# Two MLPs whose 512-column matmuls read the moving operand as two interleaved streams

## The chip, the cores and the metric

The kernel runs on one core of a Trainium2 chip. The metric is the device time of one execution in microseconds (us); the median of three runs is given. A row of the profile belongs to one profiled execution.

## The reference

Sink-and-window attention over 2 batches, 8 heads, 768 positions and 64 channels gives 1536 tokens of 512 features. Two MLPs follow, each with its own weights, 512 to 2048 to 512:

```python
x = attention(q, k, v, n_sink, window)          # (1536, 512)
h = x @ w_in;  g = h * clip(h + 3, 0, 6) / 6;  x = g @ w_out       # first MLP
h = x @ w_in2; g = h / (1 + exp(-1.702 * h));  out = g @ w_out2    # second MLP
```

All inputs and the output are float32.

## The kernel before, in words

[...] To keep the precision, each operand is split into a high part (a rounded copy) and a low part (the rest), and each product is made of three matmuls: high by high, high by low, low by high. The helper `copy` (lines 428 to 432) makes high parts on ScalarE or VectorE; the subtractions for low parts are at lines 517, 579, 637 and 850.

Tokens are taken in blocks of 512 and the 2048 hidden features in 16 pieces of 128. One *item* is one block with one piece. `up` (line 524) multiplies the block's activations by a piece of W_in: 4 chunks of 128 input features with 3 matmuls each, at line 536, into one PSUM bank of 128 hidden features by 512 tokens. The activation and the split into `gh` and `gl` follow. `down` (line 587) multiplies the result by a piece of W_out, 4 times 3 matmuls at line 604. So an item has 24 matmuls, each with a stationary operand of 128 by 128 and a moving operand of 128 by 512. There are 48 items in each MLP, 96 in all, which makes 2304 such matmuls.

What moves and what stands still differs. In `up` of both MLPs, W_in is stationary and the activations `xyh`/`xyl` (tokens along the columns) move. In `down` of the first MLP, W_out is stationary and `gh`/`gl` move, so that tokens stay along the columns. In `down` of the second MLP, `gh`/`gl` are stationary and W_out moves, so that tokens come out along the partitions and features along the columns, ready for the store at line 649. Before the change each moving operand is read from its first column to its last.

Each weight arrives as a float64, seen as two 32-bit words, and is put together as float32 by one ScalarE instruction (line 448) and four VectorE instructions (lines 453, 461, 469, 476), a piece (128 by 1024) at a time. Each piece of the first MLP's weights is kept in `wf` and replaced by the second's while the last block of the first MLP runs.

The order on every engine is written by a planner (`Plan`, line 284). Each operation has prices in ns, one for each engine that may do it, a due time and its dependencies; `issue` (line 354) places operations one after the other by start time, price and due time, and lets casts and copies fall to ScalarE or VectorE. For three matmuls of 512 columns its price is

```python
[("PE", 3 * (n / 2.4 + 13.3))]
```

that is 226.6 ns a matmul. In the fast path, the due times of successive items lie 5440 ns apart (times 1.6 or 1.25 for the first 24), at line 907. At the start of the program the attention's operations share the engines with the first items.

Of the kernel before, what the change touches and what calls it, by code (L numbers as in the profile page):

```python
# [17 lines left out]
P = 128  # L18
# [11 lines left out]
RATE_DMA = 340  # L30
# [15 lines left out]
DOWN = 7000  # L46
START = 3000
RATE = 1.6
RATE2 = 1.25
# [14 lines left out]
def tile_sink_window_attention_moe_moe2(  # L64
# [13 lines left out]
    NF = w1.shape[0]  # L78
# [349 lines left out]
    def copy(eng, out, in_):  # L428
        if eng is nc.scalar:
            eng.copy(out, in_)  # L430
        else:
            eng.tensor_copy(out, in_)  # L432

    def halves(t0, n):
        return range(t0 // 256, (t0 + n) // 256)

# [46 lines left out]
    def plan_mlps(plan, blocks, item_due):  # L483
# [40 lines left out]
        def up(i):  # L524
            which, t0, n, f = items[i][:4]
            wh, wl = split(i, 0)
            h = Buf(cls="bank", kind="h")
            s, o = divmod(t0, 512)
            for c in range(NC):

                def mm(e, c=c):
                    xh, xl = xyh[s][:, c, o : o + n], xyl[s][:, c, o : o + n]
                    cols = slice(c * P, (c + 1) * P)
                    prods = ((wh.tile[:, cols], xh), (wh.tile[:, cols], xl), (wl.tile[:, cols], xh))
                    for k, (w, x) in enumerate(prods):
                        e.matmul(  # L536
                            h.tile[:, :n], w, x, start=(c == 0 and k == 0), stop=(c == NC - 1 and k == 2)
                        )

                xs = [b for half in halves(t0, n) for b in plan.x[half][c]]  # L540
                plan.op([("PE", 3 * (n / 2.4 + 13.3))], mm, due[i], reads=[wh, wl] + xs, writes=[h], chain="up")
            u, gh, gl = (Buf(cls=x) for x in ("u", "gh", "gl"))
            big = n == 512
            after = due[i] + (2600 if big else 1300)
            if which == 1:
                plan.op(
                    [("ACT", 585 if big else 370)],
                    lambda e: e.activation(u.tile[:, :n], h.tile[:, :n], AF.Relu, bias=three, scale=1.0),  # L548
                    after, reads=[h], writes=[u],
                )  # L550
                plan.op(
                    [("DVE", 602 if big else 335)],
                    lambda e: e.scalar_tensor_tensor(  # L553
                        out=u.tile[:, :n], in0=u.tile[:, :n], scalar=6.0, in1=h.tile[:, :n],
                        op0=ALU.min, op1=ALU.mult,
                    ),
                    after, reads=[h], writes=[u],
                )
            else:
                plan.op(  # L560
                    [("ACT", 478)],
                    lambda e: e.activation(u.tile[:, :n], h.tile[:, :n], AF.Sigmoid, scale=1.702),  # L562
                    after, reads=[h], writes=[u],
                )
                plan.op(
                    [("DVE", 602)],
                    lambda e: e.tensor_tensor(
                        out=u.tile[:, :n], in0=h.tile[:, :n], in1=u.tile[:, :n], op=ALU.mult
                    ),
                    after, reads=[h], writes=[u],  # L570
                )
            plan.op(
                [("ACT", 520 if big else 307), ("DVE", 335 if big else 200)],
                lambda e: copy(e, gh.tile[:, :n], u.tile[:, :n]),
                after, reads=[u], writes=[gh],
            )
            plan.op(
                [("DVE", 602 if big else 335)],
                lambda e: e.tensor_tensor(  # L579
                    out=gl.tile[:, :n], in0=u.tile[:, :n], in1=gh.tile[:, :n].bitcast(F32), op=ALU.subtract  # L580
                ),
                after, reads=[u, gh], writes=[gl],
            )
            g[i] = (gh, gl)
            wo[i] = split(i, 1)

        def down(i):
            which, t0, n, f, begin, end = items[i]
            wh, wl = wo.pop(i)
            gh, gl = g.pop(i)  # L590
            if begin:
                ys["b"] = [Buf(cls="bank", kind="y") for _ in range(4)]
            for e4 in range(4):
                yb = ys["b"][e4]

                def mm(e, e4=e4, yb=yb):
                    col = slice(e4 * P, (e4 + 1) * P)
                    if which == 1:
                        a, b = wh.tile[:, col], wl.tile[:, col]
                        prods = ((a, gh.tile), (b, gh.tile), (a, gl.tile))  # L600
                    else:
                        prods = ((gh.tile[:, col], wh.tile), (gh.tile[:, col], wl.tile), (gl.tile[:, col], wh.tile))
                    for k, (l, r) in enumerate(prods):
                        e.matmul(yb.tile, l, r, start=(begin and k == 0), stop=(end is not None and k == 2))  # L604

                plan.op(
                    [("PE", 3 * (n / 2.4 + 13.3))], mm, due[i] + DOWN,
                    reads=[wh, wl, gh, gl], writes=[yb], chain="down",
                )
                if end == "aside":  # L610
                    keep = Buf(cls="aside")
                    kept_y[t0, e4] = keep
                    plan.op(
                        [("ACT", 478), ("DVE", 602)], lambda e, yb=yb, keep=keep: copy(e, keep.tile, yb.tile),
                        due[i] + 5200, reads=[yb], writes=[keep],
                    )
                elif end == "y":
                    result(which, t0, e4, yb, due[i] + 5200)

        def result(which, t0, e4, yb, when):  # L620
            if which == 1:
                s = t0 // 512
                hi, lo = xyh[s][:, e4, :], xyl[s][:, e4, :]
                his = [plan.x[half][e4][0] for half in halves(t0, 512)]
                los = [plan.x[half][e4][1] for half in halves(t0, 512)]
                if (t0, e4) in kept_y:
                    part, psum = kept_y[t0, e4], yb
                    plan.op(
                        [("DVE", 602)],
                        lambda e: e.tensor_tensor(out=part.tile, in0=psum.tile, in1=part.tile, op=ALU.add),  # L630
                        when, reads=[psum], writes=[part],
                    )
                    yb = part
                plan.op([("ACT", 478)], lambda e: e.mul(hi, yb.tile, 1.0 / 6.0), when, reads=[yb], writes=his)
                plan.op(
                    [("DVE", 602)],
                    lambda e: e.scalar_tensor_tensor(
                        out=lo, in0=yb.tile, scalar=1.0 / 6.0, in1=hi.bitcast(F32), op0=ALU.mult, op1=ALU.subtract,
                    ),
                    when, reads=[yb] + his, writes=los,  # L640
                )
            else:
                o = Buf(cls="u")
                plan.op(
                    [("ACT", 478), ("DVE", 602)], lambda e: copy(e, o.tile, yb.tile), when, reads=[yb], writes=[o]
                )
                r = t0 + e4 * P
                plan.op(
                    [("SP", 262144 / RATE_DMA)], lambda e: e.dma_start(out=out[r : r + P, :], in_=o.tile), when,
                    reads=[o], chain="dma",  # L650
                )

# [214 lines left out]
    def fast_path():  # L867
        with tc.manual_schedule(), tc.tile_pool(name="mlp", bufs=1) as pool, tc.tile_pool(
# [34 lines left out]
            def item_due(items):  # L903
                t, due = RAMP0 + first * RAMP + START, []
                for n in range(len(items)):
                    due.append(t)
                    t += 5440 * (RATE if n < 8 else RATE2 if n < 24 else 1)
                return due

            plan_attention(plan, ap, pair_due)  # L910
# [3 lines left out]
    def general_path():  # L914
        with ExitStack() as st:
# [75 lines left out]
            with tc.manual_schedule():  # L991
                pool = st.enter_context(tc.tile_pool(name="gmlp", bufs=1))
                psum = st.enter_context(tc.tile_pool(name="gpsum", bufs=1, space=PSUM))
                plan = Plan()
                mlp_rings(plan, pool, psum)
                plan.limit = lambda b, slots, o: b.kind == "y" or H_BANKS > sum(
                    1 for x in slots if x is not None and (x.left or x in o.new) and x.kind == "h"
                )
                plan_mlps(
                    plan, [(s * 512, 0, NF) for s in range(NBLK)], lambda items: [5200 * n for n in range(len(items))]  # L1000
                )
                plan.issue()

# [69 lines left out]
```

## Time and profile before

| | us |
|---|---|
| median of 3 runs | 623.67 |
| lowest, highest of the runs | 622.96, 623.98 |
| profiled execution, first to last instruction | 622.8 |
| TensorE busy in it | 605.6 |
| weight loads busy (they overlap the matmuls) | 500.4 |
| VectorE busy | 501.1 |
| ScalarE busy | 261.2 |
| DMA, share of the 16 engines' span (main queue) | 23.6% |

The profiled execution's time is given by its span alone, 622.8 us, 0.9 us under the median of the runs. Busy time on TensorE overstates its work, since matmuls are pipelined: one lasts about 390 ns from its start to its modelled end, and the next starts well before that. The distance from one start to the next has to be read from counts over a stretch or from the chain of waits.

### The profile page before, as it was taken

How to read it: one execution, taken by the hardware profiler on the slowest of the kernel's cores; microseconds unless marked ns; L12 is line 12 of the kernel's file. 1: busy time of each engine (PE TensorE's matmuls, PEld its weight loads, DVE VectorE, ACT ScalarE, POOL GpSimd, SP SyncE). 2: the span in 40 equal slices, each digit the busy share in tenths (PEclk: the TensorE clock that was granted, in tenths of full speed). 3: DMA queues.
4: the chain of work that ended last, by engine and by line, in shares of the span. 5: the costliest groups of instructions: out<-in, count | busy, mean ns of one | idle time of the engine just before them, and what ended most of it. 6: DMA issues, size and time to landing. Idle time of an engine off the chain costs nothing.

```text
span 622.8 us, 10596 instructions
## 1 busy us (share of the span) xinstructions
PE 605.6 (97%) x4242; PEld 500.4 (80%) x4242; DVE 501.1 (80%) x1061; ACT 261.2 (42%) x553; POOL 1.4 (0%) x10
## 2 busy tenths in 40 slices
PE   7889999999999999999999999999999999999996
PEld 6777887777888888888888888888888888888885
DVE  7799999899956686799999999966666666666753
ACT  5897887767546321164443554312311012211111
POOL 0000000000000000000000000000000000000000
PEclk8899999999999999999999999999999999999999
DMA  8974442554400000003343334000100000100001
GB/s 264 374 228 145 160 165 86 174 170 175 157 1 2 1 1 1 0 2 135 136 144 129 132 130 141 1 0 1 69 1 1 0 1 0 69 0 1 0 1 72
DMA packets 11175, 50.91 MB, mean 82 GB/s; under 512 B 1456, under 2 KB 1456, under 8 KB 7024
## 3 DMA queue, kind: packets, MB, share of 16 engines
q1 hardware_dynamic: 11120, 50.18, 23.6%
q8 instruction: 35, 0.57, 0.4%
q14 instruction: 20, 0.16, 0.1%
HBM read 47.02 MB, written 3.15 MB: 81 GB/s over the span
## 4 chain that ended last, share of the span: by engine, by line
PE 78%; DVE 13%; ACT 3%; DMA 3%; issue 2%; POOL 0%; ACTq 0%; SPq 0%; POOLq 0%
PE bank L536 37%; PE bank L604 36%; DMA stage<-in_w_dram 2%; DVE pexp L764 2%; DVE wf L476 2%; DVE wf L469 2%; PE bank L800 2%; PE bank L749 1%; ACT pexp L772 1%; DVE u L553 1%; PE bank L823 1%; DVE wf L453 1%; PE bank L831 1%; DVE wf L461 1%; DVE w1l L517 1%
## 5 line engine op out<-in xcount | busy, mean ns | idle before, releaser
L536 PE MATMUL bank<-xyh,w0h 128*128 128x512 f32 x384 | 151.8, 395 | 2.3 <-DVE u L553 1.5
L536 PE MATMUL bank<-xyl,w0h 128*128 128x512 f32 x384 | 149.6, 390 | 1.0 <-DVE xyl L850 1.0
L536 PE MATMUL bank<-xyh,w0l 128*128 128x512 f32 x384 | 149.7, 390 | 0.0
L562 ACT ACTIVATE u<-bank 128x512 f32<-128x512 f32 x48 | 28.7, 599 | 173.2 <-PE bank L536 173.2
L536 PEld LDWEIGHTS bank<-xyh,w0h 128*128 128x128 f32 x384 | 72.1, 188 | 17.9 <-DVE u L553 2.1
L536 PEld LDWEIGHTS bank<-xyl,w0h 128*128 128x128 f32 x384 | 72.1, 188 | 15.5 <-DVE xyl L850 1.3
L536 PEld LDWEIGHTS bank<-xyh,w0l 128*128 128x128 f32 x384 | 72.1, 188 | 15.4 <-DVE w0l L517 0.3
L604 PE MATMUL bank<-gh,w1h 128*128 128x512 f32 x192 | 76.4, 398 | 0.0
L604 PE MATMUL bank<-gh,w1l 128*128 128x512 f32 x192 | 74.9, 390 | 0.7 <-DVE w1l L517 0.7
L604 PE MATMUL bank<-gl,w1h 128*128 128x512 f32 x192 | 75.0, 390 | 0.1
L604 PE MATMUL bank<-w1h,gl 128*128 128x512 f32 x192 | 74.8, 390 | 0.0
L604 PE MATMUL bank<-w1l,gh 128*128 128x512 f32 x192 | 74.7, 389 | 0.0
L604 PE MATMUL bank<-w1h,gh 128*128 128x512 f32 x192 | 74.7, 389 | 0.0
L432 DVE CAST w0h<-wf 128x512 fp32r<-128x512 f32 x81 | 34.3, 424 | 46.4 <-PE bank L536 46.4
L517 DVE TENSOR_TENSOR w0l<-wf,w0h 128x512 fp32r<-128x512 f32 x96 | 66.2, 689 | 5.1 <-PE bank L604 0.5
L579 DVE TENSOR_TENSOR gl<-u,gh 128x512 fp32r<-128x512 f32 x96 | 66.2, 689 | 1.9
L517 DVE TENSOR_TENSOR w1l<-wf,w1h 128x512 fp32r<-128x512 f32 x96 | 66.1, 689 | 1.0
L548 ACT ACTIVATE u<-bank,three 128x512 f32<-128x512 f32 x48 | 33.0, 687 | 72.5 <-PE bank L536 72.3
L432 DVE CAST w1h<-wf 128x512 fp32r<-128x512 f32 x61 | 26.0, 426 | 33.1 <-PE bank L604 33.0
L772 ACT ACTIVATE pexp<-pexp,nb 128x196 f32<-128x196 f32 x96 | 43.2, 452 | 12.4 <-DVE nb L764 12.2
L448 ACT ACTIVATE wf<-stage 128x1024 f32<-128x1024 f32 x32 | 36.9, 1152 | 18.1 <-DMA stage<-in_w_dram 16.2
L430 ACT CAST gh<-u 128x512 fp32r<-128x512 f32 x47 | 29.2, 622 | 35.8 <-DVE u L553 19.8
(93 smaller groups left out, 834.8 us busy)
## 6 DMA issues: line engine op xcount, KB each, us to landing
stage<-in_w_dram SPq DMA_DIRECT2D x32, 1024.0 KB, 4.9
wf<-in_kq_dram SPq DMA_DIRECT2D x8, 520.0 KB, 11.1
vc<-in_vc_dram SPq DMA_DIRECT2D x12, 320.0 KB, 4.6
out_dram<-u SPq DMA_DIRECT2D x12, 256.0 KB, 2.0
vb<-in_v_dram SPq DMA_DIRECT2D x10, 256.0 KB, 6.3
kq<-in_kq_dram SPq DMA_DIRECT2D x4, 520.0 KB, 10.9
vb<-in_v_dram SPq DMA_DIRECT2D x4, 128.0 KB, 6.5
par_i<-in_params_dram SPq DMA_DIRECT2D x1, 2.0 KB, 2.9
```

Source lines behind the costliest of these rows:

```text
L430: eng.copy(out, in_)
L432: eng.tensor_copy(out, in_)
L448: lambda e: e.activation(w.tile.bitcast(F32), top.bitcast(F32), AF.Abs),
L469: lambda e: e.scalar_tensor_tensor(out=w.tile, in0=top, scalar=-0x40000000, in1=w.tile, op0=ALU.bitwise_and, op1=ALU.bitwise_or),
L476: lambda e: e.scalar_tensor_tensor(out=w.tile, in0=low, scalar=29, in1=w.tile, op0=ALU.logical_shift_right, op1=ALU.bitwise_or),
L517: lambda e: e.tensor_tensor(out=lo.tile, in0=src.tile.bitcast(F32)[:, cols], in1=hi.tile.bitcast(F32), op=ALU.subtract),
L536: e.matmul(h.tile[:, :n], w, x, start=(c == 0 and k == 0), stop=(c == NC - 1 and k == 2))
L548: lambda e: e.activation(u.tile[:, :n], h.tile[:, :n], AF.Relu, bias=three, scale=1.0),
L562: lambda e: e.activation(u.tile[:, :n], h.tile[:, :n], AF.Sigmoid, scale=1.702),
L579: lambda e: e.tensor_tensor(out=gl.tile[:, :n], in0=u.tile[:, :n], in1=gh.tile[:, :n].bitcast(F32), op=ALU.subtract),
L604: e.matmul(yb.tile, l, r, start=(begin and k == 0), stop=(end is not None and k == 2))
L772: lambda e, n=n: e.activation(pes[n].tile[:, :W], pes[n].tile[:, :W], AF.Exp, bias=nbs[n].tile, scale=-1.0, accum_out=z.tile[:, n : n + 1],),
```

## The change: two streams

Every matmul of the MLPs reads its 512 moving columns in another order: 0, 256, 1, 257, 2, 258, and so on. The number of columns, the instructions, the tiles and the stationary operands stay. The output is still written from the first column of the bank to the last, so its columns come out in the order of the reading.

Three such readings (`up`, `down` of the first MLP, `up` of the second) put the tokens of a block into another order: place 8r + l holds token 64l + r. The store of each 128-by-512 result writes partition 8h + l to row 64l + 16q + h of the block for the q-th of its four results, in rows of 2 KB as before. In the second MLP's `down` it is the features that come out in the order of the reading, and the host has laid W_out's columns apart for that: even columns first, odd columns after. The planner's price of a matmul falls from n/2.4 + 13.3 to n/2.4 + 2.7 ns, and the distance of the due times from 5440 to 5184 ns (5200 to 5184 in the general path, which doesn't run with these inputs).

```diff
+    def woven(x):
+
+        return x.rearrange("p (a n) -> p n a", a=2)
...
-                            h.tile[:, :n], w, x, start=(c == 0 and k == 0), stop=(c == NC - 1 and k == 2)
+                            h.tile[:, :n], w, woven(x), start=(c == 0 and k == 0), stop=(c == NC - 1 and k == 2)
...
-                plan.op([("PE", 3 * (n / 2.4 + 13.3))], mm, due[i], reads=[wh, wl] + xs, writes=[h], chain="up")
+                plan.op([("PE", 3 * (n / 2.4 + 2.7))], mm, due[i], reads=[wh, wl] + xs, writes=[h], chain="up")
...
-                        e.matmul(yb.tile, l, r, start=(begin and k == 0), stop=(end is not None and k == 2))
+                        e.matmul(yb.tile, l, woven(r), start=(begin and k == 0), stop=(end is not None and k == 2))
...
-                    [("PE", 3 * (n / 2.4 + 13.3))], mm, due[i] + DOWN,
+                    [("PE", 3 * (n / 2.4 + 2.7))], mm, due[i] + DOWN,
...
-                r = t0 + e4 * P
+                rows = out[t0 : t0 + 512, :].rearrange("(l q h) d -> q h l d", l=8, q=4)[e4]
                 plan.op(
-                    [("SP", 262144 / RATE_DMA)], lambda e: e.dma_start(out=out[r : r + P, :], in_=o.tile), when,
+                    [("SP", 262144 / RATE_DMA)],
+                    lambda e: e.dma_start(out=rows, in_=o.tile), when,
...
-                    t += 5440 * (RATE if n < 8 else RATE2 if n < 24 else 1)
+                    t += 5184 * (RATE if n < 8 else RATE2 if n < 24 else 1)
...
+    def apart(w):
+
+        return w.reshape(-1, w.shape[1] // 2, 2).transpose(0, 2, 1).reshape(w.shape)
...
-        "w2": by_tile(x["moe2_w_in"], x["moe2_w_out"]),
+        "w2": by_tile(x["moe2_w_in"], apart(x["moe2_w_out"])),
```

## Rows read from the trace of the kernel before

**Rows 1.** Stages: length, each engine's busy us (instructions), clock, DMA share, GB/s

```profile
40.00:147.93 107.93, 103.54 (x1156) 84.10 (x1151) 105.31 (x265) 82.98 (x204) 0.00 (x0) 1.00 0.47 155
290.00:400.00 110.00, 110.00 (x486) 90.55 (x485) 109.05 (x167) 50.99 (x74) 0.00 (x0) 1.00 0.35 123
400.00:616.12 216.12, 216.12 (x955) 178.97 (x954) 144.78 (x264) 35.42 (x59) 0.00 (x0) 1.00 0.03 10
```

**Rows 2.** TensorE's waits, 147 to 617 us: total us, times, longest

```profile
PE bank L536 <- ACT pts L430: 0.2, 1, 0.2
```

**Rows 3.** Chain of waits, 400 us to the end: start, us, what

```profile
525.02 2.72 PE bank L604 x12
...
531.83 4.76 PE bank L536 x21
...
616.12 2.19 DMA out_dram<-u
```

**Rows 4.** Timeline of one `up` chunk and one `down` triple: start, us, what

```profile
608.50 0.39 PE L536 MATMUL bank<-xyh,w0h 128*128 128x512 f32 x1
608.51 0.19 PEld L536 LDWEIGHTS bank<-xyl,w0h 128*128 128x128 f32 x1
608.73 0.39 PE L536 MATMUL bank<-xyl,w0h 128*128 128x512 f32 x1
...
609.18 0.39 PE L604 MATMUL bank<-w1h,gh 128*128 128x512 f32 x1
```

**Rows 5.** Eight attention transposes of 128 columns (line 800): length, PE, weight loads, clock

```profile
53.25:54.12 0.87, 0.87 (x8) 0.79 (x7) 1.00 0.00 0
```

**Rows 6.** Matmuls of line 536, stages of the whole kernel

```profile
40.00:147.93 107.93, 41.54 (x156) 28.29 (x157) 1.00 0.47 155
147.93:211.81 63.88, 29.32 (x109) 19.86 (x110) 1.00 0.17 62
211.81:290.00 78.19, 44.02 (x178) 33.22 (x178) 1.00 0.05 17
290.00:400.00 110.00, 60.83 (x244) 45.19 (x242) 1.00 0.35 123
400.00:616.12 216.12, 122.29 (x468) 87.84 (x468) 1.00 0.03 10
```

**Rows 7.** Matmuls of line 604, the same stages

```profile
40.00:147.93 107.93, 39.00 (x144) 26.04 (x144) 1.00 0.47 155
147.93:211.81 63.88, 28.62 (x108) 20.05 (x108) 1.00 0.17 62
211.81:290.00 78.19, 41.99 (x168) 31.55 (x168) 1.00 0.05 17
290.00:400.00 110.00, 60.41 (x242) 45.37 (x243) 1.00 0.35 123
400.00:616.12 216.12, 126.25 (x487) 91.13 (x486) 1.00 0.03 10
```

**Rows 8.** VectorE's casts, 290 to 400 us, by line and form

```profile
L432 DVE CAST w0h<-wf 128x512 fp32r<-128x512 f32 x17 | 7.2, 422 | 0.0
...
L432 DVE CAST w1h<-wf 128x512 fp32r<-128x512 f32 x6 | 2.6, 426 | 0.0
...
L432 DVE CAST gh<-u 128x512 fp32r<-128x512 f32 x3 | 1.3, 422 | 0.0
```

**Rows 9.** Who waits for TensorE, 400 to 616 us: total us, times, longest

```profile
ACT u L562 <- PE bank L536: 164.7, 40, 5.6
DVE w0h L432 <- PE bank L536: 32.9, 23, 2.0
DVE w1h L432 <- PE bank L604: 30.6, 16, 2.9
```

**Rows 10.** The end of the timeline: start, us, what

```profile
616.12 3.23 SPq L649 DMA_DIRECT2D out_dram<-u  x4
...
617.12 0.39 PE L604 MATMUL bank<-w1h,gl 128*128 128x512 f32 x1
618.41 0.59 ACT L430 COPY u<-bank 128x512 f32<-128x512 f32 x1 [0.96 <-DMA out_dram<-u]
```

**Rows 11.** DMA issues of the page, stores: count, KB each, us to landing

```profile
out_dram<-u SPq DMA_DIRECT2D x12, 256.0 KB, 2.0
```

More of the change, by code (lines that the diff above doesn't have):

```diff
@@ L999, in general_path @@
                 plan_mlps(
-                    plan, [(s * 512, 0, NF) for s in range(NBLK)], lambda items: [5200 * n for n in range(len(items))]
+                    plan, [(s * 512, 0, NF) for s in range(NBLK)], lambda items: [5184 * n for n in range(len(items))]
                 )
```

## The prediction

> **What bounds the kernel now.** I begin with the busy time by stages. TensorE is busy without a break from 290 us to 616 us, VectorE in 109.05 of 110 us of the one stage and in 144.78 of 216.12 us of the next [rows 1]. A busy TensorE proves little, because a matmul's 390 ns overlap the next one's. So the second view is TensorE's waits: from 147 us to 617 us it waited 0.2 us in all [rows 2]. The third is the chain of waits over the same time. It runs through TensorE's matmuls alone, and its pieces give the distance between two matmuls: 2.72 us for 12 and 4.76 us for 21, both 226.7 ns [rows 3]. The fourth, the timeline, shows the same 0.22 to 0.23 us between neighbours, and each weight load starting beside the matmul before the one that it serves and lasting 0.19 us [rows 4]. The reader is to see that for 468 us (147.93 to 616.12) nothing but the number of matmuls and their distance sets the end. Before that it is different: from 40 us to 147.93 us VectorE is busy for 105.31 of 107.93 us, with TensorE at 103.54 [rows 1]. That stage ends when VectorE is done with attention and weights.
>
> **What could be taken off a matmul.** [...]
>
> The trace has one other dense row of full-height matmuls, the attention's transposes at the same clock: 8 in 0.87 us, 108.8 ns for 128 columns [rows 5]. [...]
>
> **Part by part.** (1) *The order of reading.* [...] No row shows neighbouring columns 1 KB apart, so a loss can't be excluded either: its upper bound is taken from the slowest pace per column that a full-height matmul shows, the transposes' 108.8 / 128 = 0.85 ns, which gives 435 ns for 512 columns, 208 ns more than now. [...]
>
> [...]
>
> (2) *Where the gain counts.* From 147.93 us on, lines 536 and 604 have 109 + 178 + 244 + 468 and 108 + 168 + 242 + 487 matmuls, 2004 together [rows 6, 7]. At 11.2 ns each that is 22.4 us, all on the path. Between 40 and 147.93 us there are 156 + 144 = 300, worth 3.4 us at most, but VectorE sets that stage: the bounds are 0 and 3.4 us, and I take 0.8 us, nearer to none, since VectorE has 2.6 us of air there [rows 1, 6, 7].
>
> (3) *What is late next.* The same items now want their VectorE work in less time. From 290 us to 400 us TensorE's 486 matmuls shrink by 5.4 us to 104.6 us, while VectorE is busy for 109.05 us: a shortfall of 4.4 us if nothing moves. What can move: 26 casts on VectorE there, 11.1 us in all, may go to ScalarE, which is busy for 50.99 of 110 us [rows 1, 8]; and conversions of the second MLP's weights can slip beyond 400 us, where VectorE is idle for a third of the time and its casts wait for TensorE, 32.9 and 30.6 us [rows 1, 9]. The planner knows both ways, and its due times and price go down with the change. So the give-back lies between 0 and 4.4 us; I take 1.2 us. After 400 us an item's 5.44 us holds 3.6 us of VectorE work (67%), and 5.17 us still hold it.
>
> (4) *Stores, layout, planner.* The stores move the same 12 times 256 KB in rows of 2 KB, and land 2.0 us after issue [rows 11]. Only the last ones are on the path: 5.7 us lie between the start of the last matmul (617.12) and the end (622.8) [rows 10]. The scattered rows need one more dimension in the access pattern; if each of the four last stores took half its landing time longer and they overlapped, that is 1 us, and I take 0, keeping 0 to 1 us. The first eight stores hide behind the matmuls; nothing queues behind them on SP but the later ones. The host's layout is outside the timed program. No instruction, tile or wait is added. The planner will place another order in the first 148 us; I allow 1.5 us either way for it.
>
> **The sum.** 22.4 + 0.8 − 1.2 = 22.0 us. The profiled execution's 622.8 us becomes 600.8 us; the median of the runs lies 0.9 us above that execution's span, so the time is 601.7 us.
>
> **The rivals.** [...]
>
> [...]
>
> *A partial cure.* Half of the 11.2 ns goes: 11.6 us on the path, some 612.5 us. [...]
>
> *VectorE takes over.* The matmuls reach 215.4 ns, but all of the 4.4 us come back between 290 and 400 us and the planner loses 1.5 us early: 606.4 us. The casts in [rows 8] speak against it.
>
> **Chances and range.** Full cure 0.68 (601.7 us), VectorE taking over 0.06 (606.4), partial cure 0.06 (612.5), no change 0.07 (623.7), slower 0.13. For one launch of this kernel 0.2% is 1.2 us, about what its runs can tell from no change. Faster 0.80, same 0.06, slower 0.14 (a part of the no-change case falls out on the slow side through the planner). The range: the low end has the full 22.4 + 3.4 us and 1 us of the planner's, 623.7 − 26.8 = 596.9, say 597; the high end takes in the partial cure, 613. It leaves out no change and slower, 0.20.
>
> **What would show it.** Right: the chain of waits has 12 matmuls in about 2.59 us; TensorE's waits after 148 us stay under 2 us; the stage in which the second weights are converted holds VectorE near 100%, with fewer casts on it; transposes stay at 109 ns. [...] The prediction fails above all if the reading of columns 1 KB apart has a price of its own.

## The result, and the profile after

The changed kernel takes 616.9 us (median, 615.9 to 618.6); the kernel before took 623.8 us beside it. The ratio is 0.9899, 95% interval 0.9875 to 0.9922: faster by some 7 us, where 22 us were forecast, and outside the range of 597 to 613 us. The profiled execution spans 614.0 us against 622.8 us. Each run's time lies 1.8 to 1.9 us above its span, so the execution profiled before would have been some 624.6 us, an estimate, and longer than any of the four timed beside it, while that of after was the shortest of its runs; the two traces therefore differ by 8.8 us, more than the medians do.

The reading itself did what was forecast. The chain of waits of the changed kernel, late in the program (start, length, what), answers to [rows 3]:

```profile
519.07 2.59 PE bank L608 x12
525.54 4.53 PE bank L540 x21
```

12 matmuls in 2.59 us and 21 in 4.53 us are 215.8 ns each, 10.9 ns less than before; 215.4 had been forecast. From 410 us to the start of the last matmul TensorE works without a break, busy for all of 196.75 us with 914 matmuls, 215.3 ns each with the edges included. But the stage in which the second MLP's weights are converted shows another picture. By stages (length, then PE, weight loads, VectorE, ScalarE), before and after; the first fence is of the kernel before, cut at 410 us to match:

```profile
290.00:410.00 120.00, 120.00 (x530) 98.84 (x529) 116.45 (x180) 52.13 (x75) 0.00 (x0) 1.00 0.32 112
```

```profile
290.00:410.00 120.00, 116.66 (x519) 95.71 (x518) 118.81 (x173) 58.25 (x78) 0.00 (x0) 1.00 0.33 114
```

In these 120 us the changed kernel starts 519 matmuls, fewer than the 530 of before. At 215.8 ns there is room for 556: 37 matmuls, 8.0 us, are lost. The waits of that stage (who for whom: total us, times, longest) say to whom:

```profile
PEld bank L608 <- DVE gl L583: 8.7, 17, 0.9
PE bank L608 <- DVE gl L583: 2.6, 10, 0.5
PEld bank L608 <- ACT gh L430: 1.0, 4, 0.3
```

TensorE waits for VectorE's `gl`, again and again. And on VectorE two instructions have grown. These are the instructions that read or write the staged weights from 260 us on (ns: least, median, most), first in the kernel before, then in the changed one:

```profile
L448 ACT ACTIVATE wf<-stage x16: 1137/1150/1167, 267.4 to 388.8; 128x1024 f32<-128x1024 f32 x16
L469 DVE SCALAR_TENSOR_TENSOR wf<-stage,wf x16: 1218/1224/1230, 277.9 to 394.8; 128x1024 int32<-128x1024 int32 x16
L476 DVE SCALAR_TENSOR_TENSOR wf<-stage,wf x16: 1217/1224/1231, 280.2 to 396.2; 128x1024 int32<-128x1024 int32 x16
```

```profile
L452 ACT ACTIVATE wf<-stage x16: 1427/1619/1707, 265.5 to 401.8; 128x1024 f32<-128x1024 f32 x16
L473 DVE SCALAR_TENSOR_TENSOR wf<-stage,wf x16: 1495/1522/1589, 277.3 to 409.6; 128x1024 int32<-128x1024 int32 x16
L480 DVE SCALAR_TENSOR_TENSOR wf<-stage,wf x16: 1425/1509/1581, 281.8 to 411.6; 128x1024 int32<-128x1024 int32 x16
```

Nobody edited these lines. They have one thing in common: they take every second 32-bit word out of `stage`. The other costly instructions of both engines kept their durations within some 2% (the subtraction for `w0l` 689 and 688 ns, the sigmoid 599 and 598). In the same changed trace, before the first MLP matmul at 42 us, they still have the old length:

```profile
L452 ACT ACTIVATE wf<-stage x2: 1122/1149/1176, 19.6 to 28.4; 128x1024 f32<-128x1024 f32 x2
L473 DVE SCALAR_TENSOR_TENSOR wf<-stage,wf x2: 1218/1218/1218, 27.2 to 39.5; 128x1024 int32<-128x1024 int32 x2
```

One triple of `down` shows how the loss comes about (timeline, start, us, engine, what):

```profile
302.00 0.62 ACT L430 CAST gh<-u 128x512 fp32r<-128x512 f32 x1 [2.30 <-DVE u L557]
...
302.70 0.46 PE L608 MATMUL bank<-gh,w1h 128*128 128x512 f32 x1
...
302.82 0.68 DVE L583 TENSOR_TENSOR gl<-u,gh 128x512 fp32r<-128x512 f32 x1
302.99 0.38 PE L608 MATMUL bank<-gh,w1l 128*128 128x512 f32 x1
...
303.55 0.19 PEld L608 LDWEIGHTS bank<-gl,w1h 128*128 128x128 f32 x1 [0.59 <-DVE gl L583]
303.56 0.48 PE L608 MATMUL bank<-gl,w1h 128*128 128x512 f32 x1 [0.18 <-DVE gl L583]
```

ScalarE sits idle for 2.30 us until VectorE's `u` is there, and casts `gh` only then. `gl` starts only when `gh`'s first matmul has already begun, and the third matmul comes 0.57 us after the second in place of 0.22.

The end became longer, too. The last matmul starts at 606.75 us, 10.4 us earlier than in [rows 10], but 7.3 us remain to the end instead of 5.7. The last copy waits 2.11 us for an earlier store's buffer (0.96 in [rows 10]), and the stores land after 2.9 us instead of the 2.0 in [rows 11]:

```profile
609.21 0.59 ACT L430 COPY u<-bank 128x512 f32<-128x512 f32 x1 [2.11 <-DMA out_dram<-u]
```

```profile
out_dram<-u SPq DMA_DIRECT2D x12, 256.0 KB, 2.9
```

### The profile page after: what moved, and what is told of

It is laid out like the page before. It is cut to its first block, busy times and chain, and to the rows that moved or that the text cites. A ratio compares the mean times of both kernels' runs of the same rounds, so it can differ in the third digit from the quotient of the medians.

```text
span 614.0 us, 10605 instructions
## 1 busy us (share of the span) xinstructions
PE 588.7 (96%) x4242; PEld 500.7 (82%) x4242; DVE 508.3 (83%) x1052; ACT 275.0 (45%) x562; POOL 1.4 (0%) x10
## 4 chain that ended last, share of the span: by engine, by line
PE 57%; DVE 27%; ACT 6%; DMA 5%; issue 5%; POOL 0%; SPq 0%; ACTq 0%; DVEq 0%; POOLq 0%
PE bank L608 26%; PE bank L540 25%; DMA stage<-in_w_dram 4%; DVE wf L480 4%; DVE wf L473 4%; DVE w0l L521 3%; DVE w1l L521 3%; DVE gl L583 3%; DVE u L557 2%; ACT pexp L778 2%; PE bank L806 2%; DVE wf L457 2%; PE bank L755 2%; DVE pexp L770 2%; DVE wf L465 2%
## 5 line engine op out<-in xcount | busy, mean ns | idle before, releaser
L540 PE MATMUL bank<-xyh,w0h 128*128 128x512 f32 x384 | 147.4, 384 | 0.9 <-ACT xyh L430 0.5
L540 PE MATMUL bank<-xyl,w0h 128*128 128x512 f32 x384 | 145.6, 379 | 1.0 <-DVE xyl L856 1.0
L540 PE MATMUL bank<-xyh,w0l 128*128 128x512 f32 x384 | 145.7, 380 | 0.3 <-DVE w0l L521 0.2
L540 PEld LDWEIGHTS bank<-xyh,w0h 128*128 128x128 f32 x384 | 72.6, 189 | 11.6 <-ACT w0h L430 0.8
L540 PEld LDWEIGHTS bank<-xyh,w0l 128*128 128x128 f32 x384 | 72.6, 189 | 11.3 <-DVE w0l L521 1.1
L608 PE MATMUL bank<-gh,w1h 128*128 128x512 f32 x192 | 75.0, 390 | 1.5 <-ACT gh L430 1.2
L608 PE MATMUL bank<-w1h,gh 128*128 128x512 f32 x192 | 72.9, 380 | 0.0
L608 PE MATMUL bank<-gh,w1l 128*128 128x512 f32 x192 | 72.8, 379 | 0.0
L608 PE MATMUL bank<-w1l,gh 128*128 128x512 f32 x192 | 72.8, 379 | 0.0
L432 DVE CAST w0h<-wf 128x512 fp32r<-128x512 f32 x77 | 32.5, 422 | 33.4 <-PE bank L540 33.3
L452 ACT ACTIVATE wf<-stage 128x1024 f32<-128x1024 f32 x32 | 48.1, 1504 | 21.5 <-DMA stage<-in_w_dram 20.7
L778 ACT ACTIVATE pexp<-pexp,nb 128x196 f32<-128x196 f32 x96 | 43.1, 454 | 10.6 <-DVE nb L770 10.4
L608 PEld LDWEIGHTS bank<-gl,w1h 128*128 128x128 f32 x192 | 36.2, 189 | 13.9 <-DVE gl L583 9.2
## 6 DMA issues: line engine op xcount, KB each, us to landing
kq<-in_kq_dram SPq DMA_DIRECT2D x4, 520.0 KB, 10.9
```

Source lines behind the costliest of these rows:

```text
L452: lambda e: e.activation(w.tile.bitcast(F32), top.bitcast(F32), AF.Abs),
L540: e.matmul(h.tile[:, :n], w, woven(x), start=(c == 0 and k == 0), stop=(c == NC - 1 and k == 2))
L608: e.matmul(yb.tile, l, woven(r), start=(begin and k == 0), stop=(end is not None and k == 2))
L778: lambda e, n=n: e.activation(pes[n].tile[:, :W], pes[n].tile[:, :W], AF.Exp, bias=nbs[n].tile, scale=-1.0, accum_out=z.tile[:, n : n + 1],),
```

## The experiments

Theory A: TensorE's reading of columns 1 KB apart lengthens the instructions that read every second word from SBUF, and VectorE's lateness in the converting stages follows from that. Theory B: VectorE simply has too little time for an item once the matmuls are shorter, or the planner's new order is a bad one. All lines are numbered as in each kernel.

**Neighbouring words in the two VectorE reads**, on the changed kernel (e1) and on the kernel before (e2). The weights get other signs and low bits than the reference's, of the same size as before.

```diff
-                out=w.tile, in0=top, scalar=-0x40000000, in1=w.tile, ...
+                out=w.tile, in0=st.tile[:, 1024:], scalar=-0x80000000, in1=w.tile, ...
...
-                out=w.tile, in0=low, scalar=29, in1=w.tile, ...
+                out=w.tile, in0=st.tile[:, :1024], scalar=29, in1=w.tile, ...
```

> The changed kernel, but the two VectorE instructions that take words out of stage read 1024 neighbouring words instead of every second word (the weights get wrong signs and low bits, so the output is not the reference's). Theory A (the woven reading on TensorE slows instructions that read every second word from SBUF, and VectorE's lateness in the converting stages comes from that): both back from 1.50 to about 1.22 us, the ScalarE instruction that still reads every second word stays at 1.5 to 1.6 us, TensorE's waits for VectorE between 290 and 410 us under 2 us, matmuls at 215.8 ns, time 602 to 608 us. Theory B (VectorE simply has too little time for an item when the matmuls are shorter; the slower conversions are a side effect): 612 to 618 us.

> The kernel before with the same two VectorE reads of neighbouring words (wrong signs and low bits of the weights): the control for the run above. Both theories: these instructions stay at 1.22 us, matmuls at 226.7 ns, time 623 to 625 us. If neighbouring words alone made them shorter, the run above could not be read as planned.

Measured: e1 605.4 us, ratio to the kernel before 0.9709 (95% interval 0.969 to 0.9728); e2 623.8 us, ratio 0.9999 (0.9986 to 1.0013). In e1 the same kind of row as above reads:

```profile
L452 ACT ACTIVATE wf<-stage x32: 1131/1569/1647, 19.4 to 390.8; 128x1024 f32<-128x1024 f32 x32
L473 DVE SCALAR_TENSOR_TENSOR wf<-stage,wf x32: 1214/1219/1227, 26.4 to 398.4; 128x1024 int32<-128x1024 int32 x32
L480 DVE SCALAR_TENSOR_TENSOR wf<-stage,wf x32: 1214/1219/1228, 33.0 to 400.1; 128x1024 int32<-128x1024 int32 x32
```

The two changed reads are back at 1.22 us; ScalarE's, left as it was, stays at 1.57. In e2 both are at 1.22 us, as in the kernel before. TensorE starts 552 matmuls between 290 and 410 us. Reading neighbouring words is worth 11.5 us beside the new reading and nothing beside the old one. Theory A holds: it is the longer reads that make VectorE late; between 290 and 410 us TensorE's weight loads wait for `gl` for 0.3 us in e1, for 8.7 us in the changed kernel. The form of theory B in which VectorE's load is too large in any case falls. What ScalarE's longer read costs was not run by itself.

**The planner's prices alone**: the changed kernel with the old price and due times (e3), and the kernel before with the new ones (e4).

```diff
-    3 * (n / 2.4 + 2.7)        # e3; e4 the other way round, on the kernel before
+    3 * (n / 2.4 + 13.3)
-    t += 5184 * ...
+    t += 5440 * ...
```

> The changed kernel with the planner's old price (n/2.4 + 13.3) and old distance of due times (5440). Theory A: conversions still at 1.5 to 1.6 us and VectorE still late, time 613 to 620 us. Theory B, in the form that the new prices pack too much before the items: the planner's order again leaves VectorE its room, time under 608 us.

> The kernel before (plain reading, plain stores) with the planner's new price and due times alone. Theory A: conversions at 1.22 us, matmuls at 226.7 ns, time 622 to 626 us. Theory B, in the form that the order costs: 626 us or more, with TensorE waiting for VectorE by more than 3 us after 148 us.

Measured: e3 624.2 us, 1.0003 (0.9988 to 1.0018); e4 623.2 us, 0.9989 (0.9974 to 1.0003). e4 is as theory A expected. e3 missed both expectations. It reads as the changed kernel does, its conversions take 1.52 us, and it gives back the whole gain; between 290 and 410 us TensorE waits more, not less:

```profile
PEld bank L608 <- DVE gl L583: 12.5, 18, 1.3
PE bank L608 <- DVE gl L583: 5.4, 13, 0.9
PEld bank L608 <- ACT gh L430: 4.3, 9, 0.7
```

So the order planned with the old price is worse for the new durations than the order planned with the new one. That pointed to the third price in the plan, the conversions' own.

**Prices that the conversions have now**, on the changed kernel (e5) and, as a control, on the kernel before (e9).

```diff
-            [("ACT", 1036)],
+            [("ACT", 1480)],
...
-            [("DVE", 1135)],          # both instructions
+            [("DVE", 1420)],
```

> The changed kernel, with the planner's prices of the three instructions that read every second word of stage raised to what the changed trace shows (ScalarE 1036 to 1480 ns, VectorE 1135 to 1420 ns). Theory A1 (the harm is partly that the order is planned for shorter conversions, so that what TensorE waits for stands behind them): TensorE's waits for gl halve, time 608 to 613 us. Rival A2 (VectorE's time itself is short in the converting stages, whatever the order): 615 to 618 us.

> The kernel before (plain reading, plain stores, old price of a matmul) with the raised prices of the three conversion instructions alone: the control for the run with raised prices. If the raised prices only repair what the woven reading does to the conversions, nothing is to be had here: TensorE stays the bound at 226.7 ns, time 621 to 625 us. If raised prices make a better order by themselves, 612 to 620 us.

Measured: e5 601.2 us, 0.964 (0.9618 to 0.9662), better than theory A1's 608 to 613; e9 622.6 us, 0.9992 (0.9962 to 1.0023). The conversions of e5 are as long as in the changed kernel, VectorE is as full from 290 to 410 us, and yet the matmuls lose almost nothing:

```profile
L473 DVE SCALAR_TENSOR_TENSOR wf<-stage,wf x32: 1194/1517/1556, 26.4 to 406.2; 128x1024 int32<-128x1024 int32 x32
L480 DVE SCALAR_TENSOR_TENSOR wf<-stage,wf x32: 1204/1510/1574, 33.8 to 410.0; 128x1024 int32<-128x1024 int32 x32
```

```profile
290.00:410.00 120.00, 119.89 (x555) 104.20 (x554) 119.16 (x172) 63.99 (x88) 0.00 (x0) 1.00 0.30 106
```

555 of 556 matmuls, with VectorE busy for 119.16 of 120 us and ScalarE for 64.0 in place of 58.3. What the prices changed is how VectorE's work is spread over the items. From the first to the last start of L473 after 255 us, 16 of them, the changed kernel, e3 and e5 show (length, then PE, weight loads, VectorE, ScalarE):

```profile
277.30:409.60 132.30, 128.64 (x573) 106.04 (x572) 131.11 (x190) 63.73 (x84) 0.00 (x0) 1.00 0.32 112
278.00:403.40 125.40, 117.84 (x514) 94.58 (x514) 124.78 (x177) 59.49 (x77) 0.00 (x0) 1.00 0.34 118
270.90:406.20 135.30, 135.19 (x625) 117.62 (x624) 134.43 (x195) 71.29 (x97) 0.00 (x0) 1.00 0.30 109
```

With 24 matmuls to an item, the same conversions stand among 23.9, 21.4 and 26.0 items, and VectorE is busy for 5.49, 5.83 and 5.16 us an item. The 24 matmuls of an item take 5.18 us at 215.8 ns. So in the changed kernel, and more so in e3, VectorE has more work for an item than fits beside its matmuls, and TensorE waits; 0.31 us over 23.9 items is 7.4 us, an estimate, near the 8.0 us lost. In e5 the work just fits, as it does in e1 with its shorter reads (5.15 us an item, by the same count).

VectorE's time was short, but by the order of the plan and not whatever the order, as rival A2 had it. The price of a matmul, with the due times, moves the conversions too: between its 16 conversions the kernel before has 516 matmuls, and e4, with the new price, 569. The planner also moves casts: 31 stand on VectorE in this stretch of the changed kernel, 27 in that of e5. What the wider spacing and the moved casts are worth each was not run apart. The prices do nothing for the kernel before.

**The stores.** e6 is the changed kernel with the stores of before (the rows of a block come out in the order of the reading); e10 is e5 with the results in four unused buffers (`cls="aside"`) instead of the three shared ones (`cls="u"`).

```diff
-                rows = out[t0 : t0 + 512, :].rearrange("(l q h) d -> q h l d", l=8, q=4)[e4]
+                rows = out[t0 + e4 * P : t0 + (e4 + 1) * P, :]
```

> The changed kernel with the stores of before: each result goes to 128 neighbouring rows, so that the rows of a block stand in the order of the reading and not in the reference's. If the scattered rows cost what the end of the changed trace shows, the time from the last matmul's start to the end goes from 7.3 back to 5.6 to 5.9 us, and the total falls by 1 to 2 us to some 615.3 us. Rival (the longer end comes from elsewhere): still 7.3 us, 616 to 618 us.

> The changed kernel with the raised prices, and the results on their way to the store in the four buffers that the second MLP leaves unused, in place of the three that the activations share. If the last copy's wait for an earlier, scattered store lengthens the end, that wait is gone, the end falls from 7.3 to 5.0 to 6.3 us and the time to 599 to 600.5 us. Rival (the last store's own landing sets the end): 7.0 us or more, time 601 us as with the prices alone.

Measured: e6 615.1 us, 0.9863 (0.9839 to 0.9887). Its stores land after 2.0 us, the last copy waits 1.52 us, and 6.4 us remain after the last matmul: the landing is explained, about 1 of the 1.6 us at the end too, but the interval of its ratio overlaps that of the changed kernel. e10: 601.1 us, 0.9629 (0.9598 to 0.966). The wait of the last copy is gone and the end is some 6 us in its trace, for 7.3 in that of e5, but the time is that of e5, 601.2 us. The wait is real; that removing it shortens the program is not shown.

**What it is about the two streams.** Turns of 2 and of 4 columns (e7, e8), four streams of 128 columns (e11), and two streams with turns of one column at smaller distances (e12 to e15, e17, e18). W_out is laid apart to match in each. All have the plain stores of e6, so that e6 is what they are to be compared with; all but e13 leave the rows in another order than the reference's. The diffs are of one line:

```diff
-        return x.rearrange("p (a n) -> p n a", a=2)
+        return x.rearrange("p (a n f) -> p n a f", a=2, f=2)     # e7; f=4 in e8
+        return x.rearrange("p (a n) -> p n a", a=4)              # e11
+        return x.rearrange("p (g a n) -> p g n a", a=2, n=32)    # e12; n=4, 16, 128 in e13 to e15, 2 in e17, 64 in e18
```

> The changed kernel reading the two streams in turns of 2 columns (8 bytes) in place of 1, with W_out laid out for it and plain stores (rows not in the reference's order). If the gain needs a change of stream at each column, matmuls go back towards 226.7 ns and the time to 620 us or more. If the gain needs two streams in any turns and the harm comes from visiting another place for each 4 bytes, matmuls stay at 215.8 ns, the conversions fall below 1.4 us, and the time is 605 to 612 us.

> The same in turns of 4 columns (16 bytes). If the harm comes from visiting another place for each 4 bytes, the conversions are at 1.22 us as in the kernel before. If two streams in any turns give the gain, matmuls stay at 215.8 ns and the time is 601 to 606 us; if the gain needs the change at each column, matmuls are at 222 to 227 ns and the time is 615 to 624 us.

> The changed kernel reading four streams of 128 columns in turn (plain stores, rows not in the reference's order, W_out laid out for it). If the gain comes from changing the place at each column, matmuls stay at 215 to 217 ns and the time is 614 to 618 us. If it needs just two streams, or if each column's visit elsewhere has a price as in the runs with turns of 2 and 4 columns, matmuls are at 227 ns or more, up to 427, and the time is above 625 us.

> The changed kernel with two streams 32 columns (128 bytes) apart in place of 256 columns (1 KB), turns of one column, plain stores, rows not in the reference's order. If the distance does not matter: 215.8 ns a matmul, conversions at 1.5 us, 613 to 617 us. If the two streams must lie in far places: 227 ns or more, time above 622 us.

> Two streams 4 columns (16 bytes) apart within each 8 columns, turns of one column. Three such readings give the tokens their own order again, so the stores are those of before. If any two streams in turn give the gain and only far distances harm the conversions: 215.8 ns, conversions at 1.22 us, 599 to 602 us. If streams so near count as one run: 226.7 ns and 621 to 625 us.

> Two streams 16 columns (64 bytes) apart, plain stores, rows not in the reference's order. Same two readings: 215.8 ns and 599 to 602 us, or a distance in between at which the gain begins: 216 to 227 ns, 600 to 625 us.

> Two streams 128 columns (512 bytes) apart, plain stores, rows not in the reference's order. If the harm to the conversions grows with distance, they lie between 1.22 and 1.50 us. If it belongs to the distance of 1 KB alone, they are at 1.22 us and the time is 599 to 602 us with matmuls at 215.8 ns. If all far streams harm: 1.5 us and 613 to 617 us.

> Two streams 2 columns (8 bytes) apart within each 4 columns, plain stores, rows not in the reference's order. If two streams need no distance at all, 215.8 ns and 599 to 603 us; if both streams must lie in different groups of 16 bytes, 226.7 ns or more and 621 us or more.

> Two streams 64 columns (256 bytes) apart, plain stores, rows not in the reference's order. The harm begins between 128 and 512 bytes: if at 256 bytes, conversions at 1.5 us and 613 to 617 us; if not yet, 1.22 us and 599 to 602 us.

Measured (the pace from each chain of waits, the conversions as the median of the first VectorE one, L473):

| run | reading | ns a matmul | conversion, ns | us | ratio, 95% interval |
|---|---|---|---|---|---|
| before | in a row | 226.7 | 1222 | 623.8 | |
| e17 | streams 8 bytes apart | 226.7 | 1220 | 624.1 | 1.0 (0.9979 to 1.0021) |
| e13 | 16 bytes | 215.8 | 1219 | 602.0 | 0.9647 (0.9612 to 0.9683) |
| e14 | 64 bytes | 215.8 | 1218 | 601.2 | 0.9638 (0.96 to 0.9675) |
| e12 | 128 bytes | 215.8 | 1223 | 600.5 | 0.9619 (0.9602 to 0.9636) |
| e18 | 256 bytes | 215.8 | 1516 | 615.0 | 0.9856 (0.9828 to 0.9884) |
| e15 | 512 bytes | 215.8 | 1512 | 615.1 | 0.9856 (0.9821 to 0.989) |
| e6 | 1 KB | 215.8 | 1510 | 615.1 | 0.9863 (0.9839 to 0.9887) |
| e7 | 1 KB, turns of 2 | 333 | 1220 | 864.9 | 1.3873 (1.3843 to 1.3904) |
| e8 | 1 KB, turns of 4 | 250 | 1472 | 674.0 | 1.0817 (1.0792 to 1.0843) |
| e11 | four streams | 283 | 1220 | 749.8 | 1.2005 (1.1981 to 1.2029) |

As examples of the two measured columns, a piece of the chain of waits of e7 (12 matmuls in 4.00 us), and the reads of `stage` in e13 from 260 us on:

```profile
510.48 4.00 PE bank L540 x12
```

```profile
L452 ACT ACTIVATE wf<-stage x16: 1139/1152/1164, 260.7 to 388.8; 128x1024 f32<-128x1024 f32 x16
L473 DVE SCALAR_TENSOR_TENSOR wf<-stage,wf x16: 1214/1218/1226, 272.5 to 396.3; 128x1024 int32<-128x1024 int32 x16
```

Of the readings tried, those with two streams in turns of one column, 16 bytes to 1 KB apart, have the gain, 215.8 ns at every one of these distances; at 8 bytes it is 226.7 ns. The harm to VectorE's conversions is absent up to 128 bytes (1223 ns) and there at 256 bytes (1516 ns), and no larger at 512 bytes and 1 KB (1512 and 1510 ns). In e12 to e18 the distance is also the length that a stream runs before it jumps, and the two were not varied apart. Gain and harm are separate, and the distance chosen by the change has both. e7, e8 and e11 show that the slower case, to which the forecast gave 0.13, is no fancy: these orders cost 23 to 107 ns a matmul. e11 met its second expectation; e7 and e8 met none in its numbers, for neither a pace slower than that of reading in a row nor a slower one at shorter turns had been thought of.

**Near streams with the output in order.** Three readings with n=4 turn each 8 tokens back into their own order, so e13 needs no other store than that of before. With n=32 (e16) rows stand in another order within 64, and each result was stored by two transfers of 64 rows.

```diff
-                rows = out[t0 : t0 + 512, :].rearrange("(l q h) d -> q h l d", l=8, q=4)[e4]
+                for half in range(2):
+                    r = t0 + e4 * P + half * HALF
+                    rows = out[r : r + HALF, :].rearrange("(l h) d -> h l d", l=8)
```

> Two streams 32 columns apart as in the run with near streams, with rows and features put in the reference's order: each result is stored by two transfers of 64 rows. Conversions at 1.22 us, matmuls at 215.8 ns, the end 6 to 7.5 us after the last matmul's start, 600 to 602.5 us. Rival: the doubled stores cost more than 1.5 us at the end, above 602.5 us.

e16 takes 605.7 us, 0.9702 (0.9665 to 0.974): as the rival expected. The last copy waits 3.29 us for a store's buffer and 9.6 us remain after the last matmul. e13, 602.0 us, is the version to keep. It beats both kernels, without scattered stores and without the raised prices:

```diff
-        return x.rearrange("p (a n) -> p n a", a=2)
+        return x.rearrange("p (g a n) -> p g n a", a=2, n=4)
...
-                rows = out[t0 : t0 + 512, :].rearrange("(l q h) d -> q h l d", l=8, q=4)[e4]
+                rows = out[t0 + e4 * P : t0 + (e4 + 1) * P, :]
...
-        return w.reshape(-1, w.shape[1] // 2, 2).transpose(0, 2, 1).reshape(w.shape)
+        return w.reshape(-1, 64, 4, 2).transpose(0, 1, 3, 2).reshape(w.shape)
```

Between 290 and 410 us its TensorE starts 554 matmuls, and its longest wait for VectorE is 0.5 us.

## Why the prediction was wrong

**What bounds the kernel, and part (1), the reading: right.** No run shows the 11.2 ns a matmul that the sum takes, nor the 215.4 ns that goes with it; the runs showed 226.7 ns for reading in a row and 215.8 ns for two streams in turns of one column 1 KB apart, 10.9 ns less. What the gain comes from is not shown either: two streams in turns of 2 or 4 columns and four streams are slower than reading in a row (333, 250 and 283 ns in e7, e8 and e11), and a distance of 8 bytes gives nothing (226.7 ns in e17).

**Part (2), where the gain counts: half right.** From 410 us on all of it counted. Up to 215 us none did: both kernels start 531 MLP matmuls between 40 and 215 us (line by line 276 + 255 before, 273 + 258 after), where 3.2 us had been forecast. Here too conversions run beside attention, in 1.49 us (median of either VectorE line from 42 to 170 us). In e13, with conversions of 1.22 us, 552 MLP matmuls start by 215 us.

**Part (3), what is late next: the step that failed.** The mechanism was the right one, VectorE late in the converting stage, but its price was 1.2 us, at most 4.4, and it measured 8.0 us in that stage beside the 3.2 us early. The prediction had put TensorE's waits after 148 us under 2 us; the trace has 8.7 us for weight loads and 2.6 us for matmuls that wait for `gl`, in that stage alone. The bound had been worked out from VectorE's busy time of before, as if its instructions would keep their lengths. Every row of VectorE was taken as a constant. That VectorE's load leaves TensorE's pace alone is shown for the kernel before: 226.3 ns a matmul, edges included, with VectorE busy for 109.05 of 110 us and for 144.78 of 216.12 us [rows 1]; the reverse, that TensorE's reading leaves VectorE's instructions alone, was silently used beside it and shown by no row. In its place the runs showed a chain of three links: with streams 256 bytes to 1 KB apart, reads of every second word are longer, by 24% on VectorE and 41% on ScalarE in the changed kernel's late stage (1224 to 1522 ns and 1150 to 1619 ns; e1, and the table); the order is written for the old lengths and gives VectorE 5.49 us of work for an item of 5.18 us (e5); TensorE then waits for `gl`. Taking away the first link (e1, e12 to e14) or the second (e5) gives 600 to 605 us. The sentence "the planner knows both ways" was wrong for the reason that the planner knows only its prices.

**Part (4), stores: under-sized.** 0 us was taken, with a bound of 1 us; the end grew by 1.6 us in the trace, because the stores landed 0.9 us later and the last copy waits for an earlier one's buffer.

**The sum.** After 215 us there are 1773 matmuls; at 10.9 ns they are worth 19.3 us. Less the 8.0 us this is 11.3 us; between 215 and 290 us another 0.8 us is lost (344 matmuls where 347.5 had room), which leaves 10.5, and the last matmul did start 10.4 us earlier; less 1.6 us at the end, 8.8 us between the two traces. The 0.9 us that the prediction put between span and time is 1.75 to 2.15 us in the runs measured since.

**The rivals.** VectorE taking over was named, with a chance of 0.06 and a price too small by half. No change and a slower pace, to which the forecast gave 0.07 and 0.13, came true for other readings (226.7 ns in e17; 333, 250 and 283 ns in e7, e8 and e11), not for this one. The time, 616.9 us, lies nearest the partial cure's 612.5 (its own terms give 612.1, 623.7 less 11.6), but not in its way: 10.9 ns went, not half of the 11.2.

## What to carry to other kernels

When one engine's access pattern changes, the lengths of other engines' instructions may change, as they did here (VectorE's conversions from 1.22 to 1.52 us): look in the new trace for untouched lines that grew. A hand-written or planned order is only as good as its prices, so after such a change the prices of all instructions that grew have to be measured again; here that alone was worth 15.7 us (616.9 to 601.2). Try the same order of reading at several distances before building layout and stores around one.

## What was not expected of the hardware

Reading the 512 moving columns in a row, TensorE took 226.7 ns a matmul, and 215.8 ns when it alternated column by column between two places 16 bytes to 1 KB apart (e12 to e15, e18, e6). In the runs with places 256 bytes to 1 KB apart, other engines' reads of every second 32-bit word took longer: 1.51 us instead of 1.22 on VectorE and 1.58 instead of 1.15 on ScalarE (medians of e15), while VectorE's reads of neighbouring words took 1.22 us in e1, as in e2. At 64 and 128 bytes VectorE's kept 1.22 us and ScalarE's took 1.17 and 1.18 (e14, e12). With the slower orders of e7 and e11 VectorE's stayed at 1.22 us, with that of e8 it took 1.47. Why the step lies between 128 and 256 bytes, and by what way TensorE's reading reaches the other two engines, stays open.
